# Attention followed by an MLP on one core: one dealt list of TensorE instructions for a slot's value products, transposes and scores

## The chip, the core and the metric

The kernel runs on one core of a Trainium2 chip, as one launch. The time is that of the launch on the device in microseconds (us); lower is better. The core has five engines that run side by side, each with its own instruction queue: TensorE (PE in the profile; it multiplies matrices and transposes), VectorE (DVE), ScalarE (ACT), GpSimd (POOL) and SyncE (SP, which here only starts transfers). Engines wait for each other through semaphores. A product on TensorE is two instructions in the trace: a load of the stationary operand ("weights", on the row PEld), and a matmul that streams the moving operand past it (on the row PE). Products write to PSUM, which this kernel uses as two accumulator banks of the MLP and six banks that rotate among all other tiles.

## The reference, cut to what matters

```python
# q, k, v: (8, 8, 576, 64)   f: (8, 8, 576)
scores = matmul(q, k.T) / 8
cum = cumsum(log(clip(f, 1e-4, 1)), axis=-1)
scores = where(causal, -1e9, scores + cum[..., :, None] - cum[..., None, :])
attn = exp(scores - max(scores)); attn = attn / (sum(attn) + 1e-9)
x = matmul(attn, v)                      # 64 heads, then laid out as (8, 576, 512)
xn = (x - mean(x)) / sqrt(var(x) + 1e-6) * g_ln
out = x + maximum(xn @ w_ch1, 0) @ w_ch2 # 512 -> 2048 -> 512, 4608 tokens
```

Operands are split into a high part (rounded to the format in which TensorE takes them) and a low part (the rest), and the products high x high, high x low and low x high are summed. So most products stand in the program two or three times.

## The kernel before, in words

The program is one list of slots (L770). A slot is a head `n` and a row tile `t` in 1 to 4; tile `t` holds 128 query rows, and with `t` = 1 go the head's first 64 rows as tile 0 (L295). Because of the causal mask tile `t` needs only the first 64, 192, 320, 448 or 576 keys for `t` = 0 to 4.

For each slot the letters of a string in `ORDERS` (L53) call `piece`, and each letter emits the instructions of one step. From slot 70 on the string is `WwAthQFlMSPNgreamLRDB`. Every engine runs its instructions in the order in which they are emitted. The steps that matter here:

- **A**, `av_unit` (L499): products of attention rows with v for a finished pair of row tiles; only in slots whose older tile is 2 or 4. For tile 2 they are `ph1` products with streams of 320, 256 and 128 columns and `pl1` products with 256 and 128; for tile 4 `ph2` products with four times 256 and once 128, and `pl2` products with three times 256 and once 128. A `ph` product loads 128 columns of weights (v high and v low side by side), a `pl` product 64 columns (v high alone).
- **t**, `transpose_unit` (L448): transposes of normalised rows. The rows are the weights here (64 or 128 columns loaded), and the identity streams 128 columns. Tile 1 has two transposes with 64 columns loaded and one with 128; tile 2 one and two; tile 3 one and three; tile 4 one, three, and one more into a bank of its own (`tr_4b`).
- **Q**, `qk_mm` (L363): scores of the newest tile. Each score tile is two products, `hi` x `hi` (L374) and `kl` x `xq` (L375). They load 128 columns and stream 320 (`t` = 2), 448 (`t` = 3) or twice 288 (`t` = 4). For `t` = 1 there are two score tiles: tile 0 loads 64 columns and streams 64, tile 1 loads 128 and streams 192.
- **M** and **N**, `mm1` and `mm2`: one step of the MLP. M is 12 products with 128 columns loaded and a 256-column stream (L604 to L606), N is 6 with 128 loaded and a 512-column stream (L626 to L628). N is the last TensorE work of a slot, so a 512-column stream stands ahead of the next slot's A or t; in some slots four transposes of MLP rows (`xp`, L649) stand between.
- **h** and **l** (L490, L494) take the transposes out of PSUM on ACT and DVE; **F** (L548) copies half of the value product on ACT; **S** (L388) masks the scores and takes their row extremes on DVE.

For heads from 18 on (`MOVED`, L33) the normalised rows go through a DMA into a tile `pq` before they are transposed, and a head's transposes come four slots after its scores (`LAG_MOVED`), its value products five. So a slot of head `n` with `t` = 1 holds: value products of head `n-2`, tile 4; transposes of head `n-1`, tile 1; scores of head `n`, tiles 0 and 1. With `t` = 3 it holds the value products for tile 2 of head `n-1`, the transposes of its tile 3 and the scores of tile 3. With `t` = 2 and 4 there are transposes and scores alone.

Of the kernel before, what the change touches and what calls it, by code (L numbers as in the profile page):

```python
# [9 lines left out]
F32R = mybir.dt.float32r  # L10
# [21 lines left out]
LAG, LAG_MOVED = 2, 4  # L32
# [28 lines left out]
def attn_moe(ctx: ExitStack, tc: tile.TileContext, qk, v, f, g, w1, w2, out):  # L61
    nc = tc.nc
# [9 lines left out]
    mm = nc.tensor.matmul  # L72

    def bank(name):
        return ps.tile([P, 512], F32, tag="b", bufs=6, name=name)
# [5 lines left out]
    identr = const.tile([P, P], F32R, tag="identr", name="identr")  # L81
# [3 lines left out]
    ident = identr.bitcast(F32)  # L85
# [276 lines left out]

    def qk_mm(h, t):  # L363
        q0, m, w = QT[t]
        cuts = [(0, w)] if w <= 512 else [(0, w // 2), (w // 2, w)]
        h.s = getattr(h, "s", {})
        h.s[t] = []
        for i, (a, z) in enumerate(cuts):
            sp = bank(f"s{h.n}_{t}_{i}")[:m, : z - a]
            xq, kl = h.xq[:, q0 : q0 + m], h.kl[:, a:z]  # L370
            if h.plain:
                mm(sp, xq, kl, start=True, stop=True)  # L372
            else:
                mm(sp, h.hi[:, 0, q0 : q0 + m], h.hi[:, 1, a:z], start=True, stop=False)  # L374
                mm(sp, xq, kl, start=False, stop=True)  # L375
            h.s[t].append((a, z, sp))

    corners = []

# [54 lines left out]
    def rows_of(h, t):  # L434
        return h.moved.get(t, h.p[t][0])

    def tr(out_, in_):
        m = in_.shape[0]
        if in_.dtype == F32R:
            nc.tensor.transpose(out_.bitcast(F32R), in_, identr[:m, :m])  # L440
        else:
            nc.tensor.transpose(out_, in_, ident[:m, :m])  # L442

# [2 lines left out]
    def transpose_unit(h, t):  # L448
        n = f"{h.n}"
        pt = rows_of(h, t)  # L450
        work_ = []
        if t <= 2:
            if t == 1:
                h.ph1 = work.tile([P, 704], F32 if h.full else F32R, tag="ph1", bufs=1, name=f"ph1_{n}")
                h.pl1 = None if h.full else late.tile([P, 384], F32R, tag="pl1", bufs=1, name=f"pl1_{n}")
            ph = h.ph1
            pl = ph if h.full else h.pl1
            tp = bank(f"tr{n}_{t}")
            if t == 1:
                tr(tp[0:64, 0:128], rows_of(h, 0)[:, 0:D])  # L460
                tr(tp[0:64, 64:192], pt[:, 0:64])
                tr(tp[:, 192:320], pt[:, 64:192])
                work_.append((tp[0:64, 0:192], ph[0:64, 0:192], ph[64:128, 0:192]))
                work_.append((tp[:, 192:320], ph[:, 320:448], pl[:, 0:128]))
            else:
                tr(tp[0:64, 0:128], pt[:, 0:64])
                tr(tp[:, 128:256], pt[:, 64:192])
                tr(tp[:, 256:384], pt[:, 192:320])
                work_.append((tp[0:64, 0:128], ph[0:64, 192:320], ph[64:128, 192:320]))
                work_.append((tp[:, 128:384], ph[:, 448:704], pl[:, 128:384]))  # L470
        else:
            if t == 3:
                h.ph2 = work.tile([P, 9 * P], F32 if h.full else F32R, tag="ph2", bufs=1, name=f"ph2_{n}")
                h.pl2 = None if h.full else late.tile([P, 7 * P], F32R, tag="pl2", bufs=1, name=f"pl2_{n}")
            c = 0 if t == 3 else P
            ph = h.ph2[:, : 8 * P].rearrange("p (k c) -> p k c", k=4)[:, :, c : c + P]
            pl = None if h.full else h.pl2[:, : 6 * P].rearrange("p (k c) -> p k c", k=3)[:, :, c : c + P]
            tp = bank(f"tr{n}_{t}").rearrange("p (k c) -> p k c", k=4)
            tr(tp[0:64, 0, :], pt[:, 0:64])
            for k in range(1, 4):  # L480
                tr(tp[:, k, :], pt[:, 64 + P * (k - 1) : 64 + P * k])
            work_.append((tp[0:64, 0, :], ph[0:64, 0, :], ph[64:128, 0, :]))
            work_.append((tp[:, 1:4, :], ph[:, 1:4, :], pl))
            if t == 4:
                tp = bank(f"tr{n}_4b")[:, :P]
                tr(tp, pt[:, 64 + 3 * P : 64 + 4 * P])
                work_.append((tp, h.ph2[:, 8 * P :], None if h.full else h.pl2[:, 6 * P :]))
        h.parts = work_

    def transposed_hi(h, t):  # L490
        for tp, hi, lo in h.parts:
            nc.scalar.copy(out=hi, in_=tp)  # L492
# [5 lines left out]

    def av_unit(h, t):  # L499
        po = bank(f"o{h.n}_{t}")  # L500

        if h.full:
            def fac(o, k, mv, first=False):
                st, mv = (h.vr[0:64, 0], mv[0:64]) if k == 0 else (h.vr[:, k], mv)
                mm(o, st, mv, start=first, stop=True, skip_group_check=True)  # L505

            if t == 2:
                ph = h.ph1
                fac(po[0:64, 0:320], 0, ph[:, 0:320], True)
                fac(po[0:64, 64:320], 1, ph[:, 320:576])  # L510
                fac(po[0:64, 192:320], 2, ph[:, 576:704])
                h.o = (po, S1, 0)
            else:
                ph = h.ph2
                for k in range(4):
                    fac(po[0:64, 0:256], k, ph[:, 256 * k : 256 * k + 256], k == 0)
                fac(po[0:64, 128:256], 4, ph[:, 8 * P :])
                h.o = (po, S - S1, S1)
            return

        vv = h.vv

        def both(k):
            return vv[:, k].rearrange("p a d -> p (a d)")

        def acc(o, st, mv, first=False):
            mm(o, st, mv, start=first, stop=True, skip_group_check=True)  # L527

        if t == 2:
            ph, pl, w, c0 = h.ph1, h.pl1, S1, 0  # L530
            acc(po[:, 0:320], both(0), ph[:, 0:320], True)
            acc(po[:, 64:320], both(1), ph[:, 320:576])
            acc(po[:, 192:320], both(2), ph[:, 576:704])
            acc(po[0:64, 64:320], vv[:, 1, 0, :], pl[:, 0:256])
            acc(po[0:64, 192:320], vv[:, 2, 0, :], pl[:, 256:384])
        else:
            ph, pl, w, c0 = h.ph2, h.pl2, S - S1, S1
            for k in range(4):
                acc(po[:, 0:256], both(k), ph[:, 256 * k : 256 * k + 256], k == 0)
            acc(po[:, 128:256], both(4), ph[:, 8 * P :])  # L540
            for k in range(1, 4):
                acc(po[0:64, 0:256], vv[:, k, 0, :], pl[:, 256 * (k - 1) : 256 * k])
            acc(po[0:64, 128:256], vv[:, 4, 0, :], pl[:, 6 * P :])
        h.o = (po, w, c0)

    xs_tile = {}

# [225 lines left out]
    hd = {}  # L773
# [12 lines left out]
    for u, slot in enumerate(slots):  # L786
# [4 lines left out]
        if slot is not None:  # L791
            n, t = slot
            h = hd[n]
        def turn(more):

            for lag in (LAG, LAG_MOVED):
                b = before(lag + more)
                if b is not None and hd[b[0]].lag == lag:
                    return b
            return None  # L800

        av, av_t = None, 0
        if turn(1) is not None and turn(1)[1] in (2, 4):
            av, av_t = hd[turn(1)[0]], turn(1)[1]
        moe.fetch_low(ALL if wp.done() else wp.ready())
        want = moe.can(wp.ready()) and u >= FIRST_MOE

        def piece(c):
            tu = turn(0)
            if c == "t" and tu is not None:  # L810
                transpose_unit(hd[tu[0]], tu[1])
            elif c == "h" and tu is not None:
                transposed_hi(hd[tu[0]], tu[1])
            elif c == "l" and tu is not None:
                transposed_lo(hd[tu[0]])
            elif c == "Q" and slot is not None:
                if t == 1:
                    qk_mm(h, 0)
                qk_mm(h, t)
            elif c == "A" and av is not None:  # L820
                av_unit(av, av_t)
            elif c == "S" and slot is not None:
                if t == 1:
                    softmax_a(h, 0)
# [65 lines left out]
        for c in [o for first, o in ORDERS if first <= u][-1]:  # L890
            piece(c)
# [48 lines left out]
```

## Time and profile before

| | |
|---|---|
| time before, median of 3 runs | 1207.02 us (1204.66 to 1209.07) |
| time of the profiled execution | 1205.75 us |
| its span, first to last instruction | 1204.0 us |
| transposes of heads from 18 on | 275.0 to 997.1 us of the span |
| POOL busy | 426.1 us |

The span has three parts: a beginning with weights being prepared and the first 18 heads, the stretch from 275 to 997 us with heads 18 to 63 and the MLP in alternation, and an end of 207 us with the MLP alone. The views used are the page, the busy times by windows, and the timeline of the two TensorE rows. In a timeline row stand the start, the duration, the engine, the line, the operation with its tiles, the rows and columns of the weights (128*64 is 64 columns loaded), the shape of the moving operand, and the count of merged instructions.

### The profile page before, as it was taken

How to read it: one execution, taken by the hardware profiler on the slowest of the kernel's cores; microseconds unless marked ns; L12 is line 12 of the kernel's file. 1: busy time of each engine (PE TensorE's matmuls, PEld its weight loads, DVE VectorE, ACT ScalarE, POOL GpSimd, SP SyncE). 2: the span in 40 equal slices, each digit the busy share in tenths (PEclk: the TensorE clock that was granted, in tenths of full speed). 3: DMA queues.
4: the chain of work that ended last, by engine and by line, in shares of the span. 5: the costliest groups of instructions: out<-in, count | busy, mean ns of one | idle time of the engine just before them, and what ended most of it. 6: DMA issues, size and time to landing. Idle time of an engine off the chain costs nothing.

```text
span 1204.0 us, 25987 instructions
## 1 busy us (share of the span) xinstructions
PE 1185.4 (98%) x8140; PEld 1057.7 (88%) x8140; DVE 756.5 (63%) x2884; ACT 643.2 (53%) x1920; POOL 426.1 (35%) x533
## 2 busy tenths in 40 slices
PE   7998999999999999999999999999999999999998
PEld 5666889999999999989999999999999999999997
DVE  5787647676768676766767676767676764233232
ACT  5888655565656565556565555556565642112111
POOL 3568544343434434344434433434444320000000
PEclk8999999999999999999999999999999999999999
DMA  7788653557666767567676666657666654434433
GB/s 204 228 239 272 204 163 118 154 172 214 219 202 202 234 187 231 170 217 218 212 224 199 209 207 205 221 181 231 199 220 213 189 182 135 128 121 126 139 108 94
DMA packets 171481, 228.50 MB, mean 190 GB/s; under 512 B 40784, under 2 KB 107856, under 8 KB 171344
## 3 DMA queue, kind: packets, MB, share of 16 engines
q1 hardware_dynamic: 171344, 226.85, 60.7%
q8 instruction: 65, 1.06, 0.4%
q14 instruction: 72, 0.59, 0.1%
HBM read 157.46 MB, written 23.36 MB: 150 GB/s over the span
## 4 chain that ended last, share of the span: by engine, by line
PE 92%; DVE 3%; ACT 2%; DMA 2%; issue 1%; SPq 0%; POOL 0%; DVEq 0%; ACTq 0%; POOLq 0%
PE h L604 11%; PE h L605 11%; PE h L606 11%; PE acc L626 11%; PE acc L627 11%; PE acc L628 11%; PE o L527 6%; PE s L374 4%; PE tr L440 4%; PE s L375 3%; PE o L505 3%; PE tr L442 2%; PE s L372 2%; PE xp L649 1%; PE pc L191 1%
## 5 line engine op out<-in xcount | busy, mean ns | idle before, releaser
L416 POOL TENSOR_SCALAR p<-p,st 64x64 f32<-64x64 f32 (+4 forms) x320 | 172.5, 543 | 489.4 <-DVE st L415 196.7
L604 PE MATMUL h<-x,w1h 128*128 128x256 f32 x1152 | 330.0, 286 | 0.8 <-ACT xs L558 0.8
L605 PE MATMUL h<-x,w1h 128*128 128x256 f32 x1152 | 325.6, 283 | 1.4 <-DVE st L414 1.3
L606 PE MATMUL h<-x,w1l 128*128 128x256 f32 x1152 | 325.3, 282 | 0.0
L612 ACT ACTIVATE hh<-h 128x256 fp32r<-128x256 f32 x288 | 110.3, 383 | 303.3 <-PE h L606 303.0
L617 DVE SCALAR_TENSOR_TENSOR hh<-h,hh 128x256 fp32r<-128x256 f32 x288 | 121.1, 421 | 172.9 <-ACT hh L612 170.9
L626 PE MATMUL acc<-w2h,hh 128*128 128x512 f32 x576 | 226.6, 393 | 0.0
L627 PE MATMUL acc<-w2s,hh 128*128 128x512 f32 x576 | 226.4, 393 | 0.0
L628 PE MATMUL acc<-w2h,hh 128*128 128x512 f32 x576 | 225.1, 391 | 0.0
L604 PEld LDWEIGHTS h<-x,w1h 128*128 128x128 f32 x1152 | 218.8, 190 | 6.2 <-ACT xs L558 1.0
L605 PEld LDWEIGHTS h<-x,w1h 128*128 128x128 f32 x1152 | 219.2, 190 | 5.2 <-DVE x L589 2.0
L606 PEld LDWEIGHTS h<-x,w1l 128*128 128x128 f32 x1152 | 219.2, 190 | 0.0
L409 ACT ACTIVATE p<-p,st 64x64 f32<-64x64 f32 (+4 forms) x320 | 178.3, 558 | 49.2 <-DVE st L398 45.6
L492 ACT CAST ph<-tr 64x128 fp32r<-64x128 f32 (+4 forms) x416 | 117.8, 332 | 130.9 <-PE tr L440 76.5
L398 DVE CUSTOM_DVE_ANT_0 p<-s,mask 64x64 f32<-64x64 f32 (+4 forms) x320 | 130.7, 420 | 17.0 <-DMA pq<-p 5.2
L497 DVE TENSOR_TENSOR ph<-tr,ph 64x192 fp32r<-64x192 f32 x208 | 62.6, 301 | 108.7 <-ACT ph L492 83.6
L628 PEld LDWEIGHTS acc<-w2h,hh 128*128 128x128 f32 x576 | 108.2, 188 | 24.1
L626 PEld LDWEIGHTS acc<-w2h,hh 128*128 128x128 f32 x576 | 109.4, 190 | 12.6
L627 PEld LDWEIGHTS acc<-w2s,hh 128*128 128x128 f32 x576 | 109.3, 190 | 11.8
L374 PE MATMUL s<-hi 128*64 128x64 f32 x336 | 105.4, 336 | 1.3 <-POOL hi L352 1.0
L497 DVE TENSOR_TENSOR pl<-tr,ph 128x128 fp32r<-128x128 f32 x208 | 95.3, 458 | 4.6
L375 PE MATMUL s<-kl,xq 66*64 66x64 f32 x336 | 98.0, 296 | 0.0
(86 smaller groups left out, 1784.5 us busy)
## 6 DMA issues: line engine op xcount, KB each, us to landing
w2s<-w2d SPq DMA_DIRECT2D x288, 256.0 KB
raw<-in_qk_dram SPq DMA_DIRECT2D x56, 576.0 KB
wr<-in_w_dram SPq DMA_DIRECT2D x32, 512.0 KB
pq<-p SPq DMA_DIRECT2D x46, 288.0 KB
pq<-p SPq DMA_DIRECT2D x46, 224.0 KB
vr<-in_v_dram SPq DMA_DIRECT2D x64, 160.0 KB
out_dram<-xt SPq DMA_DIRECT2D x36, 256.0 KB
xq<-hi SPq DMA_DIRECT2D x56, 144.0 KB
```

The lines of the kernel that those rows point to most:

```text
L374: mm(sp, h.hi[:, 0, q0 : q0 + m], h.hi[:, 1, a:z], start=True, stop=False)
L375: mm(sp, xq, kl, start=False, stop=True)
L398: nc.vector.tensor_tensor_reduce(out=pt[:m, a:z], in0=sp, in1=mask[:m, off + a : off + z], scale=-SCALE, scalar=3.0e38 if i == 0 else st[: ...
L409: nc.scalar.activation(pt[:m, :w], pt[:m, :w], AF.Exp, bias=st[:m, i : i + 1], scale=-1.0, accum_out=st[:m, 2:3])
L416: nc.gpsimd.tensor_scalar(out=pt[:m, :w], in0=pt[:m, :w], scalar1=st[:m, 3:4], scalar2=1.0, op0=ALU.mult, op1=ALU.mult)
L497: nc.vector.tensor_tensor(out=lo, in0=tp, in1=hi.bitcast(F32), op=ALU.subtract)
L604: mm(ph, w1h[:, k, fs], c.x[k][:, 0, :], start=(k == 0), stop=False)
L605: mm(ph, w1h[:, k, fs], c.x[k][:, 1, :], start=False, stop=False)
L606: mm(ph, w1l[:, k, fs], c.x[k][:, 0, :], start=False, stop=(k == KT - 1))
L626: mm(c.acc[i], h[:, 0, ts_], w2h[:, j, :], start=(j == 0), stop=False)
L627: mm(c.acc[i], h[:, 0, ts_], low, start=False, stop=False)
L628: mm(c.acc[i], h[:, 1, ts_], w2h[:, j, :], start=False, stop=(j == FT - 1))
```

## The change

`qk_mm`, `transpose_unit` and `av_unit` no longer emit their products and transposes; each returns a list of them. For heads with the lag of four, the letter A now builds all three lists (and allocates their PSUM banks in the order of before), deals them into one list with a new function `dealt`, and emits that; the letters t and Q then emit nothing. Earlier heads run their lists as they come.

```diff
     def qk_mm(h, t):
         q0, m, w = QT[t]
+        todo = []
+
+        def mm(*a, **k):
+            todo.append(lambda: nc.tensor.matmul(*a, **k))
...
+    def dealt(t, u1, a, b, q):
+
+        if t == 4 and q:
+            return a[:5] + a[8:] + b[:2] + q[:1] + a[5:6] + b[2:] + q[1:2] + a[6:7] + q[2:3] + a[7:8] + q[3:]
+        if t == 4:
+            return a[:5] + a[8:] + b[:2] + a[5:6] + b[2:] + a[6:8]
+        if t == 2:
+            return a[:3] + a[4:] + b + a[3:4] + q
+        return (a + b if u1 else b[1:] + b[:1]) + q
...
         def piece(c):
             tu = turn(0)
-            if c == "t" and tu is not None:
-                transpose_unit(hd[tu[0]], tu[1])
+            if c in "AtQ" and tu is not None and hd[tu[0]].lag == LAG_MOVED:
+                if c == "A":
+                    a = av_unit(av, av_t) if av is not None else []
+                    b = transpose_unit(hd[tu[0]], tu[1])
+                    q = []
+                    if slot is not None:
+                        q = (qk_mm(h, 0) if t == 1 else []) + qk_mm(h, t)
+                    run(dealt(av_t, tu[1] == 1, a, b, q))
+            elif c == "t" and tu is not None:
+                run(transpose_unit(hd[tu[0]], tu[1]))
...
             elif c == "A" and av is not None:
-                av_unit(av, av_t)
+                run(av_unit(av, av_t))
```

In `dealt`, `a` are the value products, `b` the transposes, `q` the score products; its `t` is the tile of the value products (0 where there are none).

The rows below are TensorE's instructions in order: line, tile written, tiles read, and the shape of the result (partitions x columns streamed). Names carry the head: `o28_4` is the value product of head 28 for tile 4, `tr29_1` the transposes of head 29's tile 1, `s30_1_0` scores of head 30's tile 1, `h` and `acc` the MLP. First a slot with `t` = 1, on TensorE, before, from the last `ph` product on:

```order
L527 MATMUL o28_4_6646<-ph2_28_6526,vv28_6428 128x128
L527 MATMUL o28_4_6646<-pl2_28_6527,vv28_6428 64x256 x3
L527 MATMUL o28_4_6646<-pl2_28_6527,vv28_6428 64x128
L440 MATMUL tr29_1_6658<-identr_74,pq29_0_6511 64x128
L440 MATMUL tr29_1_6658<-identr_74,pq29_1_6513 64x128
L440 MATMUL tr29_1_6658<-identr_74,pq29_1_6513 128x128
L374 MATMUL s30_0_0_6664<-hi30_6422 64x64
L375 MATMUL s30_0_0_6664<-kl30_6423,xq8_1143 64x64
L374 MATMUL s30_1_0_6667<-hi30_6422 128x192
L375 MATMUL s30_1_0_6667<-kl30_6423,xq8_1143 128x192
L604 MATMUL h5_0_6675<-x5_0_6172,w1h_124 128x256
```

and the same slot with the change, from the `pl` product that comes first now:

```order
L513 MATMUL o28_4_6646<-pl2_28_6522,vv28_6428 64x128
L456 MATMUL tr29_1_6649<-identr_74,pq29_0_6511 64x128
L456 MATMUL tr29_1_6649<-identr_74,pq29_1_6513 64x128
L368 MATMUL s30_0_0_6650<-hi30_6422 64x64
L513 MATMUL o28_4_6646<-pl2_28_6522,vv28_6428 64x256
L456 MATMUL tr29_1_6649<-identr_74,pq29_1_6513 128x128
L368 MATMUL s30_0_0_6650<-kl30_6423,xq8_1143 64x64
L513 MATMUL o28_4_6646<-pl2_28_6522,vv28_6428 64x256
L368 MATMUL s30_1_0_6651<-hi30_6422 128x192
L513 MATMUL o28_4_6646<-pl2_28_6522,vv28_6428 64x256
L368 MATMUL s30_1_0_6651<-kl30_6423,xq8_1143 128x192
L628 MATMUL h5_0_6675<-x5_0_6172,w1h_124 128x256
```

The three `pl` products with 256-column streams have moved from ahead of the transposes to between transposes and scores, and the one with 128 columns stands ahead of them. Next a slot with `t` = 3 on TensorE, before, from the last `ph` product on:

```order
L527 MATMUL o29_2_6780<-ph1_29_6656,vv29_6699 128x128
L527 MATMUL o29_2_6780<-pl1_29_6657,vv29_6699 64x256
L527 MATMUL o29_2_6780<-pl1_29_6657,vv29_6699 64x128
L440 MATMUL tr29_3_6788<-identr_74,pq29_3_6639 64x128
L440 MATMUL tr29_3_6788<-identr_74,pq29_3_6639 128x128 x3
L374 MATMUL s30_3_0_6795<-hi30_6422 128x448
L375 MATMUL s30_3_0_6795<-kl30_6423,xq8_1143 128x448
```

and with the change:

```order
L513 MATMUL o29_2_6780<-ph1_29_6647,vv29_6699 128x128
L513 MATMUL o29_2_6780<-pl1_29_6648,vv29_6699 64x128
L456 MATMUL tr29_3_6783<-identr_74,pq29_3_6639 64x128
L456 MATMUL tr29_3_6783<-identr_74,pq29_3_6639 128x128 x3
L513 MATMUL o29_2_6780<-pl1_29_6648,vv29_6699 64x256
L368 MATMUL s30_3_0_6784<-hi30_6422 128x448
L368 MATMUL s30_3_0_6784<-kl30_6423,xq8_1143 128x448
```

The `pl` product with the 256-column stream has moved behind the transposes. Last a slot with `t` = 2 on TensorE, before, behind the MLP's last product:

```order
L626 MATMUL acc5_1_6760<-w2h_126,hh5_4_6953 128x512
L627 MATMUL acc5_1_6760<-w2s84_6837,hh5_4_6953 128x512
L628 MATMUL acc5_1_6760<-w2h_126,hh5_4_6953 128x512
L440 MATMUL tr30_2_6970<-identr_74,pq30_2_6832 64x128
L440 MATMUL tr30_2_6970<-identr_74,pq30_2_6832 128x128 x2
L374 MATMUL s31_2_0_6976<-hi31_6693 128x320
L375 MATMUL s31_2_0_6976<-kl31_6694,xq9_1286 128x320
```

and with the change:

```order
L652 MATMUL acc5_1_6760<-w2h_126,hh5_4_6953 128x512
L456 MATMUL tr30_2_6970<-identr_74,pq30_2_6832 128x128 x2
L456 MATMUL tr30_2_6970<-identr_74,pq30_2_6832 64x128
L368 MATMUL s31_2_0_6971<-hi31_6693 128x320
L368 MATMUL s31_2_0_6971<-kl31_6694,xq9_1286 128x320
```

The transpose that loads 64 columns has moved behind those that load 128; `t` = 4 is dealt in the same way. The order on DVE, ACT, POOL and SP is that of before.

More of the change, by code (lines that the diff above doesn't have):

```diff
@@ L376, in qk_mm @@
             h.s[t].append((a, z, sp))
+        return todo
     corners = []
@@ L435, in rows_of @@
         return h.moved.get(t, h.p[t][0])
[L437 to L442, printed above, removed]
     def transpose_unit(h, t):
@@ L450, in transpose_unit, with tr @@
         pt = rows_of(h, t)
-        work_ = []
+        work_, todo = [], []
+        def tr(out_, in_):
+            m = in_.shape[0]
+            if in_.dtype == F32R:
+                todo.append(lambda: nc.tensor.transpose(out_.bitcast(F32R), in_, identr[:m, :m]))
+            else:
+                todo.append(lambda: nc.tensor.transpose(out_, in_, ident[:m, :m]))
         if t <= 2:
@@ L488, in transpose_unit @@
         h.parts = work_
+        return todo
     def transposed_hi(h, t):
@@ L500, in av_unit, with mm @@
         po = bank(f"o{h.n}_{t}")
+        todo = []
+        def mm(*a, **k):
+            todo.append(lambda: nc.tensor.matmul(*a, **k))
         if h.full:
@@ L518, in av_unit @@
                 h.o = (po, S - S1, S1)
-            return
+            return todo
         vv = h.vv
@@ L544, in av_unit @@
         h.o = (po, w, c0)
+        return todo
+    def dealt(t, u1, a, b, q):
[6 more added lines that the diff above has]
+        return (a + b if u1 else b[1:] + b[:1]) + q
     xs_tile = {}
@@ L806, in attn_moe, with run @@
         want = moe.can(wp.ready()) and u >= FIRST_MOE
+        def run(todo):
+            for emit in todo:
+                emit()
         def piece(c):
             tu = turn(0)
-            if c == "t" and tu is not None:
-                transpose_unit(hd[tu[0]], tu[1])
+            if c in "AtQ" and tu is not None and hd[tu[0]].lag == LAG_MOVED:
[8 more added lines that the diff above has]
+                run(transpose_unit(hd[tu[0]], tu[1]))
             elif c == "h" and tu is not None:
@@ L816, in piece @@
             elif c == "Q" and slot is not None:
-                if t == 1:
-                    qk_mm(h, 0)
-                qk_mm(h, t)
+                run((qk_mm(h, 0) if t == 1 else []) + qk_mm(h, t))
             elif c == "A" and av is not None:
-                av_unit(av, av_t)
+                run(av_unit(av, av_t))
             elif c == "S" and slot is not None:
```

## The prediction

> **What bounds the kernel now.** The page first: busy times, and the chain of work that ended last.
>
> ```profile
> span 1204.0 us, 25987 instructions
> ...
> PE 1185.4 (98%) x8140; PEld 1057.7 (88%) x8140; DVE 756.5 (63%) x2884; ACT 643.2 (53%) x1920; POOL 426.1 (35%) x533
> ...
> PE 92%; DVE 3%; ACT 2%; DMA 2%; issue 1%; SPq 0%; POOL 0%; DVEq 0%; ACTq 0%; POOLq 0%
> ```
>
> TensorE is the bound: 98% busy and 92% of the chain. Next, where the changed instructions run (the transposes' tile `pq`), and the busy times of that stretch by windows.
>
> ```profile
> L440 PE MATMUL tr<-identr,pq x644: 220/231/300, 275.0 to 997.1; 128*128 128x128 f32 x92, 128*64 128x128 f32 x69
> L440 PE MATMUL tr_4b<-identr,pq x46: 246/247/248, 286.2 to 997.2; 128*128 128x128 f32 x46
> ...
> 275.00:997.00 722.00, 719.89 (x5210) 662.98 (x5208) 507.48 (x1987) 423.94 (x1289) 284.26 (x360) 1.00 0.66 207
> ```
>
> `tr_4b` is made once a head: 46 heads. In their 722 us PE is busy 719.89, so all its waiting there is 2.1 us; the next engine, DVE, is busy 507.48, or 70%. The granted clock is 1.00. Only TensorE's own stream of instructions can move this stretch. But a busy PE row does not say that it streams all the time, so the third view is the timeline of the weight loads. A slot with `t` = 2, from the load under the MLP's last 512-column stream on:
>
> ```profile
> 626.28 0.11 PEld L440 LDWEIGHTS tr<-identr,pq 128*64 128x64 f32 x1
> 626.51 0.14 PEld L440 LDWEIGHTS tr<-identr,pq 128*128 128x128 f32 x1
> 626.60 0.14 PEld L440 LDWEIGHTS tr<-identr,pq 128*128 128x128 f32 x1
> 626.68 0.19 PEld L374 LDWEIGHTS s<-hi 128*128 128x128 f32 x1
> 626.79 0.19 PEld L375 LDWEIGHTS s<-kl,xq 66*128 66x128 f32 x1
> 626.94 0.19 PEld L604 LDWEIGHTS h<-x,w1h 128*128 128x128 f32 x1
> 627.09 0.19 PEld L605 LDWEIGHTS h<-x,w1h 128*128 128x128 f32 x1
> ```
>
> I read the start of a load as the moment when the product before it takes over the array, since only then can the next weights be loaded behind it. The distance of two starts is then the longer of two things: the stream of the product that runs, and the load that goes on behind it. 626.28 to 626.51 is the 512-column stream (0.23). 626.51 to 626.60 to 626.68 cannot be streams, as I show next, so they are loads of 128 columns for a transpose: 0.085 each. 626.68 to 626.79 is a load of 128 columns for a product: 0.11. The last two steps, 0.15, are the 320-column streams. A slot with `t` = 1 gives the other prices:
>
> ```profile
> 622.64 0.43 PEld L527 LDWEIGHTS o<-pl,vv 128*64 128x64 f32 x4
> 623.05 0.26 PEld L440 LDWEIGHTS tr<-identr,pq 128*64 128x64 f32 x3
> 623.26 0.13 PEld L374 LDWEIGHTS s<-hi 128*64 128x64 f32 x1
> 623.31 0.14 PEld L375 LDWEIGHTS s<-kl,xq 66*64 66x64 f32 x1
> 623.37 0.19 PEld L374 LDWEIGHTS s<-hi 128*128 128x128 f32 x1
> 623.48 0.19 PEld L375 LDWEIGHTS s<-kl,xq 66*128 66x128 f32 x1
> 623.59 0.19 PEld L604 LDWEIGHTS h<-x,w1h 128*128 128x128 f32 x1
> 623.71 0.19 PEld L605 LDWEIGHTS h<-x,w1h 128*128 128x128 f32 x1
> ```
>
> The transpose with 128 columns loaded takes over at 623.26 and its 128-column stream is through by 623.31: so a 128-column stream is no longer than 0.06, and the 0.085 above were loads. 623.31 to 623.37 is a load of 64 columns behind a 64-column stream: 0.057. The next three steps, 0.11 each, are loads of 128 columns behind streams of 64, 192 and 192. **Short streams with large loads behind them are where TensorE is held up.** A slot with `t` = 3 prices the streams:
>
> ```profile
> 630.54 0.13 PEld L527 LDWEIGHTS o<-pl,vv 128*64 128x64 f32 x1
> 630.60 0.13 PEld L527 LDWEIGHTS o<-pl,vv 128*64 128x64 f32 x1
> 630.72 0.11 PEld L440 LDWEIGHTS tr<-identr,pq 128*64 128x64 f32 x1
> 631.03 0.19 PEld L374 LDWEIGHTS s<-hi 128*128 128x128 f32 x1
> 631.14 0.19 PEld L375 LDWEIGHTS s<-kl,xq 66*128 66x128 f32 x1
> ```
>
> With 64 columns to load, a 128-column stream takes 0.06 (630.54 to 630.60) and a 256-column one 0.12 (630.60 to 630.72). So a load of 128 columns (0.11) is hidden behind 256 columns and sticks out 0.05 behind 128; one of 64 columns (0.057) is hidden behind 128.
>
> **The change part by part.** No instruction is added or removed; TensorE's order alone changes, in heads 18 to 63. Below, ns per step, each the longer of stream and load.
>
> *`t` = 2.* Before, from the takeover of the first transpose to that of the scores: 85 + 85 + 110 = 280 (the rows: 626.51 to 626.79). After, the first 128-column load lies behind the 512-column stream and costs nothing; then 85 (second), 60 (the 64-column one, hidden behind a 128-column stream), 110 (scores): 255. Saved 25. *`t` = 4* has two more transposes and the same ends: saved 25. That a first 128-column load vanishes behind 512 columns is seen where MLP rows are transposed:
>
> ```profile
> 629.68 0.14 PEld L649 LDWEIGHTS xp<-identr,xw 128*128 128x128 f32 x1
> 629.91 0.14 PEld L649 LDWEIGHTS xp<-identr,xw 128*128 128x128 f32 x1
> ...
> 630.08 0.14 PEld L649 LDWEIGHTS xp<-identr,xw 128*128 128x128 f32 x1
> 630.17 0.19 PEld L527 LDWEIGHTS o<-ph,vv 128*128 128x128 f32 x1
> ```
>
> 629.68 to 629.91 is the bare 0.23. By the order of the program two slots of each kind have these transposes ahead instead and save nothing: 44 slots each, 44 x 2 x 25 = 2.2 us.
>
> *`t` = 3.* Before, from the last `ph` product's takeover to that of the scores: 60 + 120 + 60 + 3 x 85 + 110 = 605 (rows: 630.54 to 631.14, 600). After: `pl` 60, transposes 60 + 3 x 85, then the `pl` product's 64 columns behind a transpose, 60, and the scores' 128 columns behind its 256, 120: 555. Against the rows that saves 45, against the steps 50; I take 47. 46 slots, 2.2 us.
>
> *`t` = 1.* Before, from the last `ph` product on: 60, 3 x 120, 60, 60, 85, 57, 57, 110, 110, 110 = 1069 (rows: 622.64 to 623.71, 1.07). After, in the order of the new rows: `pl` 60, transposes 60 and 60, score 60, `pl` behind a 64-column stream 57, transpose 120, score 60, `pl` 57, score 120, `pl` behind a 192-column stream 90 (three quarters of 120, an estimate from the 256-column step), score 120, MLP 110 = 974. Saved 95; 44 slots, 4.2 us; the last head's slot without scores some 0.1.
>
> Sum: 2.2 + 2.2 + 4.2 + 0.1 = **8.7 us**, off the path in full, since nothing else holds PE in this stretch. What is late next:
>
> ```profile
> 639.59 0.47 ACT L492 CAST ph<-tr 64x192 fp32r<-64x192 f32 x2 [0.77 <-PE s L374]
> 640.09 0.37 ACT L561 COPY ot<-o 64x256 f32<-64x256 f32 x1
> ...
> 636.54 0.28 DVE L497 TENSOR_TENSOR pl<-tr_4b,ph 128x128 fp32r<-128x128 f32 x1
> ...
> 638.73 0.58 PE L527 MATMUL o<-pl,vv 128*64 128x256 f32 x4
> ...
> L527 PE MATMUL o<-pl,vv x272: 221/278/298, 282.1 to 993.6; 128*64 128x256 f32 x136
> ```
>
> ACT's copy of the value product now waits for the last moved `pl` product. Behind it in ACT's queue stand the copy of the next head's rows, the MLP's first copy and that slot's exponentials, for which DVE and POOL wait. By the steps above that `pl` product takes over 0.68 after the first one (at 638.73 in these rows), and products of its shape last 0.28 (the last row, the median): done at about 639.7, ahead of the 640.09 at which ACT comes to the copy today; the casts ahead of it start 0.2 earlier, as the transposes do. So I cost the wait at nothing; without the cover of 0.4 ACT would lose what goes beyond 640.09, and it is 59% busy here. The `pl` product that now comes first reads what DVE ends at 636.82, 1.9 us earlier. DMAs, and the queues of SP and POOL, keep their order.
>
> Not shown before: score and value products in alternation. The bounds: nothing (tr to score took 57, no more than its load), or the whole load exposed, 57, at each added change of kind. I take nothing, the nearest rows.
>
> The whole sum rests on loads that hide behind streams: from 623.59 to 623.71 the MLP's first 256-column stream (0.12) and a load of 128 columns (0.11) pass in 0.12. The Trainium skill, "TensorE: Matmul & The Clock Gate", Part 3, "The mechanism", says that a load overlaps with a running matmul only where their row groups differ; both of these use all 128 rows and overlap, so the trace disagrees, and what the rule would give here is rival (d).
>
> **The rivals.** (a) *The transposes are slow themselves*: 85 wherever they stand, and 25 more at their end. Then `t` = 2, 3 and 4 save nothing and `t` = 1 some 70 (95 less the 25 at its transpose): 44 x 70 = 3.1 us, 1202.7. For it: the steps of `t` = 2 alone would read the same. Against it: 623.26 to 623.31.
>
> (b) *Slower: each change of kind (value product, transpose, score) exposes the load that comes with it*, in the slots with `t` = 1, which go from 3 such changes to 10, and by one in `t` = 3: 44 x 7 + 46 = 354 more. At 57 each that is 20.2 us, less 8.7: 11.5 slower, 1217.3. It decides from 25 ns a change. Against it: the changes there are (value product to transpose, transpose to score, score to MLP) show bare loads and streams.
>
> (c) *The gain is met elsewhere*: transfers or DVE hold PE as soon as it runs ahead; 1205.8. Against it: 2.1 us of waits in 722.
>
> (d) *Loads do not hide behind streams, so that order is worth nothing*: each step a sum, stream + load. The same loads and streams then add up in any order: 1205.8. Against it: 256 columns with a load of 128 would take 0.12 + 0.11, and take 0.12.
>
> **How the numbers follow.** The profiled execution took 1205.75, its span and 1.75 around it that the change does not touch; 1205.75 - 8.7 = 1197.05. It lies 1.3 below the median of 1207.02, which gives 1198.3 from there; I take the middle, **1197.7**. Chances: forecast 0.74; half the gain, with the steps in alternation longer than I think, 1201.4, 0.08; (a) 0.06; (b) 0.05; (c) 0.05; (d) 0.02. The three runs of before spread from 2.4 below to 2.0 above their median, so the forecast itself is 1195 to 1200.5; the range, with half the gain and (a), is **1195 to 1203**. A difference of 0.3% (3.6 us) is about what a measurement of this kernel can tell from no change. Faster: forecast and half, 0.82; within: (a), (c), (d), 0.13; slower: (b), 0.05.
>
> **What would show it.** The stretch of the `pq` transposes, 722 us, comes out at 713, with PE still busy all through; the 207 us behind it stay. In a slot with `t` = 1 the way from the last `ph` product to the MLP is 0.97, not 1.07, with no step over 0.12; in `t` = 3, 0.555 to the scores; in `t` = 2, the first step behind 0.23 belongs to a second 128-column transpose. Wrong would be: moved `pl` products at 0.11 or more behind 64-column streams (b), the 64-column transpose in `t` = 2 at 0.085 (a), or new waits of PE for DVE, ACT or DMA (c).

## The result, and the profile after

| | before | with the change |
|---|---|---|
| median of the runs | 1207.29 us (4 runs, 1204.66 to 1209.07) | 1199.09 us (4 runs, 1198.67 to 1200.18) |
| span of the profiled execution | 1204.0 us | 1196.9 us |

The ratio is 0.9935, with a 95% interval from 0.9916 to 0.9955: 5.4 to 10.1 us less, 7.8 in the middle. 8.7 us were forecast, and 1197.7 us.

The page and the views of the changed kernel that answer to those of before: busy times, the transposes' tile `pq`, the busy times by windows, and the waits of PE in the stretch.

```profile
span 1196.9 us, 26079 instructions
...
PE 1176.4 (98%) x8140; PEld 1050.7 (88%) x8140; DVE 758.8 (63%) x2884; ACT 643.6 (54%) x1920; POOL 426.0 (36%) x533
...
L456 PE MATMUL tr<-identr,pq x644: 220/227/280, 275.5 to 990.1; 128*128 128x128 f32 x115, 128*64 128x128 f32 x46
...
275.00:990.00 715.00, 712.25 (x5212) 656.61 (x5210) 509.45 (x1988) 424.69 (x1291) 284.34 (x360) 1.00 0.66 209
990.00:1197.00 207.00, 202.99 (x1321) 184.48 (x1318) 61.55 (x188) 38.08 (x98) 0.00 (x0) 1.00 0.40 123
...
PE h L629 <- DVE st L420: 1.0, 1, 1.0
PE tr L456 <- DMA pq<-p: 0.9, 1, 0.9
PE o L513 <- DVE ph L506: 0.4, 1, 0.4
PE s L368 <- DVE st L404: 0.3, 1, 0.3
```

The work is the same, 8140 products. The stretch of the `pq` transposes went from 722.1 to 714.6 us; the 207 us behind it stayed. PE is busy in 712.25 of 715, its waits are four, and the other engines' busy times are those of before within half a per cent. So the time came out of TensorE's own stream, though its instruction list holds the same loads and matmuls. Most of it is due to the order; up to 1 us of the 7.5 is not, as the head near 515 us shows below.

How it came out is read from the weight loads. A slot with `t` = 1 of the changed kernel, timeline of the loads (columns as before), from the first `pl` product's load on:

```profile
650.53 0.13 PEld L513 LDWEIGHTS o<-pl,vv 128*64 128x64 f32 x1
650.61 0.17 PEld L456 LDWEIGHTS tr<-identr,pq 128*64 128x64 f32 x2
650.72 0.13 PEld L368 LDWEIGHTS s<-hi 128*64 128x64 f32 x1
650.78 0.14 PEld L513 LDWEIGHTS o<-pl,vv 128*64 128x64 f32 x1
650.86 0.14 PEld L456 LDWEIGHTS tr<-identr,pq 128*128 128x128 f32 x1
650.96 0.14 PEld L368 LDWEIGHTS s<-kl,xq 66*64 66x64 f32 x1
651.02 0.14 PEld L513 LDWEIGHTS o<-pl,vv 128*64 128x64 f32 x1
651.08 0.19 PEld L368 LDWEIGHTS s<-hi 128*128 128x128 f32 x1
651.20 0.13 PEld L513 LDWEIGHTS o<-pl,vv 128*64 128x64 f32 x1
651.28 0.19 PEld L368 LDWEIGHTS s<-kl,xq 66*128 66x128 f32 x1
651.40 0.19 PEld L628 LDWEIGHTS h<-x,w1h 128*128 128x128 f32 x1
651.51 0.19 PEld L629 LDWEIGHTS h<-x,w1h 128*128 128x128 f32 x1
```

The start of a load is again read as the takeover of the product ahead of it. 650.53 is the takeover of the last `ph` product, 651.51 that of the MLP's first: 0.98, where it was 1.07 to 1.08. The 128-column loads of scores start at 651.08 and 651.28, under the 256-column streams of the `pl` products ahead of them, and the steps to the next starts are 0.12, no more than those streams. The 64-column loads behind 64-column streams are over in 0.08 (650.78 to 650.86) and 0.06 (651.02 to 651.08).

### The profile page after: what moved, and what is told of

The parts are those of the page before. It is cut to its first block, busy times and chain, and to the rows that moved or that the text cites. A ratio compares the mean times of both kernels' runs of the same rounds, so it can differ in the third digit from the quotient of the medians.

```text
span 1196.9 us, 26079 instructions
## 1 busy us (share of the span) xinstructions
PE 1176.4 (98%) x8140; PEld 1050.7 (88%) x8140; DVE 758.8 (63%) x2884; ACT 643.6 (54%) x1920; POOL 426.0 (36%) x533
## 4 chain that ended last, share of the span: by engine, by line
PE 67%; DVE 1%; DMA 1%; issue 0%; SPq 0%; DVEq 0%
PE h L628 9%; PE h L629 9%; PE h L630 9%; PE acc L650 9%; PE acc L651 9%; PE acc L652 9%; PE s L368 5%; PE o L513 5%; PE tr L456 3%; PE xp L673 1%; DMA pq<-p 1%; DVE xt L709 0%; PE tr_4b L456 0%; DVE p L404 0%; DVE pl L506 0%
## 5 line engine op out<-in xcount | busy, mean ns | idle before, releaser
L368 PE MATMUL s<-hi 128*64 128x64 f32 x336 | 101.6, 311 | 1.3 <-POOL hi L352 1.0
L368 PE MATMUL s<-kl,xq 66*64 66x64 f32 x336 | 95.5, 289 | 0.0
```

Source lines behind the costliest of these rows:

```text
L368: todo.append(lambda: nc.tensor.matmul(*a, **k))
```

## The experiments

All kernels below differ from the changed one in `dealt` alone. The ways through a slot are medians over some 35 to 43 slots of a kind, from the starts of the loads; times are compared with runs of before on the same chip. How many us less a kernel takes is worked out from the ratio, which has the interval in brackets; the difference of the two medians is up to 1.2 us away from it. Where heads are compared, a head is the time from the MLP's first load behind one slot with `t` = 1 to that behind the next, the same head in both traces, one trace for each kernel. Heads in which PE waits (near 385 and 515 us, and one near 810 us in two of the traces) are left out.

### The parts alone

First, only slots with `t` = 2 and 4 dealt:

```diff
     def dealt(t, u1, a, b, q):
 
-        if t == 4 and q:
...
-            return a[:3] + a[4:] + b + a[3:4] + q
+        if t:
+            return a + b + q
         return (a + b if u1 else b[1:] + b[:1]) + q
```

> Only the slots without value products (t = 2 and 4) are dealt: the 64-column transpose last. Theory (a load is hidden behind a long stream and sticks out behind a short one): in a t = 2 slot the way from the takeover of the first transpose to that of the scores falls from 0.28 to 0.25, in 44 slots of each kind; 2.2 to 2.7 us less than before, 1203 to 1205 by the time of before. Rival (transposes with 128 columns are slow themselves, wherever they stand): 0.28 stays, and the time of before, 1205 to 1207.

Measured: 1204.11 us against 1205.62, ratio 0.9994 (0.9981 to 1.0006). In the slots the theory held: from the takeover of the first transpose to that of the scores 0.248 instead of 0.279 with `t` = 2, and 0.417 instead of 0.452 with `t` = 4. Over the whole slots, from the takeover of the MLP's last product to that of the next step's first, medians again, it is 0.030 and 0.039, 3.0 us over 44 of each kind. (The 0.061 in an expectation below counts on to the step's third product.) So the transposes are not slow themselves: their first load is paid or hidden. But only 0.7 us of it arrived in the time, with an interval that takes in nothing; head by head it is 0.023 in the mean, 1.1 us over 46 heads. Where most of it went is seen in the MLP step behind the slot, 18 products. Timeline of the loads of this kernel: the starts that mark the takeover of the step's first product and of its last:

```profile
665.45 0.19 PEld L625 LDWEIGHTS h<-x,w1h 128*128 128x128 f32 x1
...
668.07 0.19 PEld L513 LDWEIGHTS o<-ph,vv 128*128 128x128 f32 x1
```

By these rounded rows it is 2.62, behind `t` = 4. There the median was 2.574 before, and in this kernel 36 of 45 steps take 2.61. Behind `t` = 3 it rose from 2.576 to 2.593. The slots whose order was left alone moved too: with `t` = 1 the whole slot is 0.016 shorter than before, with `t` = 3 it is 0.009 longer. So one slot's way depends by some 0.01 on what ran ahead of it.

Second, only `t` = 1 dealt: the last two returns become `return a + b + q`.

> Only the slots with t = 1 are dealt. Theory: from the takeover of the last ph product to that of the MLP 0.98 instead of 1.07 to 1.08, 44 slots, 4.0 to 4.2 us less than before, about half of what the whole change gave. Rival (the gain comes mostly from the transposes' order in the other slots): under 2 us less.

Measured: 1201.18 us, ratio 0.9964 (0.9952 to 0.9976), 4.3 us less. The slot's way is 0.98 instead of 1.08, and the MLP steps behind it kept their length. This part is more than half of the gain.

Third, only `t` = 3 dealt: the first two returns are left out, the last becomes `return a + b + q`.

> Only the slots with t = 3 are dealt. From the takeover of the last ph product to that of the scores 0.56 instead of 0.59, 1.3 us less than before by these steps. Two theories on the MLP step behind these slots, which took 2.61 instead of 2.58 in most of them with the whole change: if the dealt order of this slot makes it, it is 2.61 here too, and of the 1.3 us only some 0.5 are left; if the earlier slots make it, it stays 2.58 and 1.3 us are left.

Measured: 1204.73 us, ratio 0.9990 (0.9980 to 1.0000), 1.2 us less, with an interval that ends at nothing; head by head it is 1.2 us too. From the last `ph` product to the scores 0.560 instead of 0.590. The MLP step behind took 2.59 in 31 of 46 slots and 2.58 in 13: longer by 0.01 to 0.02, not by 0.03. So neither theory has it: the dealt order of this slot does not by itself make 2.61.

### The same alternation with spoiled pairs

```diff
         if t == 4 and q:
-            return a[:5] + a[8:] + b[:2] + q[:1] + a[5:6] + b[2:] + q[1:2] + a[6:7] + q[2:3] + a[7:8] + q[3:]
+            return a[:5] + a[5:6] + a[8:] + q[:1] + a[6:7] + b[:1] + q[1:2] + a[7:8] + b[1:2] + q[2:3] + b[2:] + q[3:]
```

> The change, but in slots with t = 1 the same products, transposes and scores stand in an order with as many changes of kind (10) and the pairs spoiled: 128-column loads stand behind 64- and 128-column streams again, and the 256-column streams are spent on 64-column loads. Theory (pairs of stream and load decide): from the last ph product to the MLP 1.07, as before the change, 4 us slower than the change. Rival (alternation as such shortens the slot, since value products no longer stand in a row): as fast as the change, 0.98. Rival (alternation costs): slower than 1.08.

Measured: 1203.38 us, ratio 0.9984 (0.9973 to 0.9996), 2 us less than before where the change gave 7.8. Timeline of the loads: takeover of the last `ph` product, then the end of the slot:

```profile
668.73 0.13 PEld L513 LDWEIGHTS o<-pl,vv 128*64 128x64 f32 x1
...
669.39 0.19 PEld L368 LDWEIGHTS s<-hi 128*128 128x128 f32 x1
669.52 0.14 PEld L456 LDWEIGHTS tr<-identr,pq 128*128 128x128 f32 x1
669.61 0.19 PEld L368 LDWEIGHTS s<-kl,xq 66*128 66x128 f32 x1
669.72 0.19 PEld L628 LDWEIGHTS h<-x,w1h 128*128 128x128 f32 x1
669.83 0.19 PEld L629 LDWEIGHTS h<-x,w1h 128*128 128x128 f32 x1
```

1.10 from 668.73 to 669.83, against 0.98 with the change and 1.08 before. The same twelve products in as many changes of kind take 0.12 longer when the 128-column loads stand behind short streams again; alternation alone gains nothing. It is 0.02 over the way of before: the load of the last transpose, behind a product of scores, starts 0.13 after that product's load and not 0.11 (669.39 to 669.52). The next experiments are about such late loads.

### Where the changed slots are longer than the sum

In the changed slot above, the step behind the first `pl` product is 0.08 (650.53 to 650.61), not 0.06. Two theories, and one edit:

```diff
-            return a[:5] + a[8:] + b[:2] + q[:1] + a[5:6] + b[2:] + q[1:2] + a[6:7] + q[2:3] + a[7:8] + q[3:]
+            return a[:5] + b[:1] + a[8:] + b[1:2] + q[:1] + a[5:6] + b[2:] + q[1:2] + a[6:7] + q[2:3] + a[7:8] + q[3:]
...
-            return a[:3] + a[4:] + b + a[3:4] + q
+            return a[:3] + b[:1] + a[4:] + b[1:] + a[3:4] + q
```

> The change, with one thing more: in slots with t = 1 and 3 the 64-column transpose stands between the last ph product and the pl product that streams 128 columns, where the change has these two products in a row. With the change the ph product's takeover to that of the pl product, and on to that of the transpose, takes 0.132 to 0.136 in the load starts, against 0.12 by the prices (two streams of 128 columns). Theory 1 (two products in a row that add to the same 128 columns of a bank hold each other up): the three steps are 0.06 each, 0.014 saved in 90 slots, 1.2 us faster than the change. Theory 2 (the load that waits for a semaphore comes late): the step over 0.06 stays with the transpose or moves with it, and nothing is saved.

Measured: 1199.36 us against 1199.30 for the change on the same chip (ratio to before 0.9946, 0.9930 to 0.9962). Nothing was saved; the slot with `t` = 3 even takes 0.01 more, and head by head this kernel saves 5.9 us where the change saves 6.8. Theory 1 falls. A `t` = 3 slot of this kernel, loads:

```profile
658.71 0.19 PEld L513 LDWEIGHTS o<-ph,vv 128*128 128x128 f32 x1
658.84 0.11 PEld L456 LDWEIGHTS tr<-identr,pq 128*64 128x64 f32 x1
658.90 0.13 PEld L513 LDWEIGHTS o<-pl,vv 128*64 128x64 f32 x1
658.98 0.31 PEld L456 LDWEIGHTS tr<-identr,pq 128*128 128x128 f32 x3
```

The transpose's load now starts 0.13 behind the `ph` product's, where 0.118 is usual there, and the next transpose's load 0.08 behind that of the `pl` product, though nothing adds to the same columns next to it any more. Nor is it the wait on a semaphore, since the load at 658.98 has none. What the late loads have in common is a transpose behind a product. But not every load of that kind is late: the first transpose of before stands behind a `pl` product too, and its load starts 0.12 after that product's (630.60 to 630.72 in the rows of the prediction), just the 256-column stream that runs there. The late loads start some 0.02 after the load ahead of them could be over: 0.08 behind a load of 64 columns (0.057), 0.13 behind one of 128 (0.11). This is a reading of these traces; no run varied the load ahead alone. One more order was tried for this, with three such places in `t` = 3:

```diff
-            return a[:3] + a[4:] + b + a[3:4] + q
+            return a[:3] + b[:1] + a[4:] + b[1:3] + a[3:4] + b[3:] + q
```

> The change, with the slots of t = 3 in an order that goes three times from a product to a transpose, twice of them behind 128-column streams: ph product, transpose (64), pl (128), transpose, transpose, pl (256), transpose, scores. Theory from the last runs (the load of a transpose that comes behind a product starts 0.02 late, which shows unless the product streams 256 columns): from the last ph product's takeover to that of the scores 0.070, 0.060, 0.105, 0.085, 0.060, 0.120, 0.110 = 0.61; loads of the first transpose and of the one behind the pl product with 128 columns start 0.015 to 0.03 after the matmul ahead of them instead of 0.003. Rival (loads and streams alone, no cost of a change of kind): 0.58. Against 0.56 with the change, so about 2 us slower than the change by the theory and 1 by the rival.

Loads of a `t` = 3 slot of that kernel:

```profile
659.07 0.19 PEld L513 LDWEIGHTS o<-ph,vv 128*128 128x128 f32 x1
659.20 0.11 PEld L456 LDWEIGHTS tr<-identr,pq 128*64 128x64 f32 x1
659.25 0.13 PEld L513 LDWEIGHTS o<-pl,vv 128*64 128x64 f32 x1
659.33 0.23 PEld L456 LDWEIGHTS tr<-identr,pq 128*128 128x128 f32 x2
659.50 0.13 PEld L513 LDWEIGHTS o<-pl,vv 128*64 128x64 f32 x1
659.58 0.14 PEld L456 LDWEIGHTS tr<-identr,pq 128*128 128x128 f32 x1
659.68 0.19 PEld L368 LDWEIGHTS s<-hi 128*128 128x128 f32 x1
659.79 0.19 PEld L368 LDWEIGHTS s<-kl,xq 66*128 66x128 f32 x1
```

The `ph` product takes over at 659.19 (659.07 and a 256-column stream of 0.12), the scores at 659.79: 0.60 to 0.61, as the theory of late loads had it, not 0.58. (The medians give 0.605: 0.59 from the first transpose's load on, and the 0.014 by which that load is late.) All three loads of transposes behind products come late (0.13 for 0.118, twice 0.08 for 0.06), and only the one behind 256 streamed columns costs nothing: from 659.50 to 659.68, 0.18, is a 64-column load and a 256-column stream. The time is 1200.84 us, ratio 0.9953 (0.9933 to 0.9973); between 1 and 2 us more than the change it cannot tell. Head by head it saves 4.8 us where the change saves 6.8, the 2 us of the theory.

### What is saved in the slots of transposes, and the whole against its parts

```diff
-        return (a + b if u1 else b[1:] + b[:1]) + q
+        return (a + b if u1 else b[1:2] + b[:1] + b[2:]) + q
```

> The change, but in slots with t = 2 and 4 the 64-column transpose stands second instead of last. Theory (what is saved is the first 128-column load, behind the 512-column stream): the steps are 0.06, 0.085, 0.11 where the change has 0.085, 0.055, 0.11, from first takeover to scores 0.25, as with the change. Rival (the saving comes from having the smaller transpose ahead of the scores' load): 0.28, as before, and 2.6 us slower than the change.

Measured: 1198.15 us, ratio 0.9936 (0.9918 to 0.9955), like the change. With `t` = 2 the steps are 0.060, 0.085, 0.108, together 0.253 against 0.248 with the change and 0.279 before. The place of the small transpose hardly matters (0.005); a 128-column load under the 512-column stream does.

> The changed kernel itself once more, for a narrower interval and beside the next three: 7 to 8.5 us less than before.

Measured: 1199.30 us, ratio 0.9942 (0.9924 to 0.9959), 7.0 us less.

For the last one, `t` = 2 and 4 stand as before (`return a + b + q` at the end):

> The change without its part for t = 2 and 4, whose slots stand as before. Alone that part saved 0.061 a head in its own slots (2.7 us) and only 0.7 in the time, since the MLP steps behind t = 4 went from 2.58 to 2.61. If that loss belongs to the part, this kernel is within 1 us of the change; if the loss depends on the whole program's timing, it is 2 to 3 us slower than the change and 4.5 to 6 faster than before.

Measured: 1200.14 us, ratio 0.9956 (0.9941 to 0.9970): 5.3 us less than before. By the ratios it is 1.7 us slower than the change measured beside it, by the medians 0.8. The intervals overlap, so by the times it stays open whether the part for `t` = 2 and 4 brings 2 to 3 us or under 1 inside the whole. Head by head this kernel is 0.117 shorter than before and the change 0.149, 5.4 and 6.8 us over 46 heads: 1.4 us for the part in these two traces.

## Why the prediction was right, point by point

**The bound** held: PE alone sets this stretch, its waits are 2.75 us (2.1 before), and the 207 us behind did not move. One thing in it was overlooked: the granted clock of 1.00 is rounded. The kernel before, busy times behind a wait of PE (the third number from the end is the granted clock):

```profile
517.80:521.20 3.40, 3.40 (x17) 3.32 (x16) 1.34 (x5) 1.47 (x5) 2.61 (x3) 0.50 0.99 379
```

For 3.4 us TensorE ran at half its clock. In the first trace of the changed kernel this does not happen in the stretch; in its second trace it does, once, from 519.5 us on and for as long. Why it comes in some runs is open.

**The reading of load starts** held, and with it the prices 0.057, 0.085, 0.11, and 0.06 and 0.12 for the streams. By slot, as medians of the load starts:

| slot | forecast saving | measured, whole slot to the takeover of the MLP's first product | MLP step behind, before to after |
|---|---|---|---|
| `t` = 1 | 0.095 | 0.097 | 2.583 to 2.587 |
| `t` = 2 | 0.025 | 0.033 | 2.585, the same |
| `t` = 3 | 0.047 | 0.028 | 2.576 to 2.610 |
| `t` = 4 | 0.025 | 0.028 | 2.574 to 2.583 |
| a head | 0.192 | 0.186 | 0.047 longer |

The head's period went from 15.64 to 15.50 us, 0.14 less: 0.186 less 0.047. Heads with transposes of MLP rows in their slots gained 0.10 to 0.21 each. In the mean it is 0.149 a head, 6.8 us over 46 heads, and in the second trace of the change 6.9. The first trace's stretch gained 7.5, mostly since one more head, near 515 us, took 17.62 us before, with the half clock in it, and 16.47 with the change; in the second trace the same head took 18.59. So what the order is worth is some 6.8 us. That the time came out as near to the forecast as 7.8 is partly luck; its interval, 5.4 to 10.1, holds 6.8 as well as 8.7.

**Two terms were mis-sized.** In `t` = 3 I took 0.047 and it is 0.028. The slot whose rows I quoted had MLP transposes ahead; in an ordinary slot the way before was shorter. Loads of such a slot in the kernel before, the one that marks the `ph` product's takeover and the one that marks the scores':

```profile
677.51 0.19 PEld L527 LDWEIGHTS o<-pl,vv 128*64 128x64 f32 x2
...
678.10 0.19 PEld L375 LDWEIGHTS s<-kl,xq 66*128 66x128 f32 x1
```

The same way in the changed kernel:

```profile
657.96 0.13 PEld L513 LDWEIGHTS o<-pl,vv 128*64 128x64 f32 x1
658.04 0.36 PEld L456 LDWEIGHTS tr<-identr,pq 128*64 128x64 f32 x4
658.35 0.13 PEld L513 LDWEIGHTS o<-pl,vv 128*64 128x64 f32 x1
658.40 0.19 PEld L368 LDWEIGHTS s<-hi 128*128 128x128 f32 x1
658.52 0.19 PEld L368 LDWEIGHTS s<-kl,xq 66*128 66x128 f32 x1
```

0.59 before, not 0.60; 0.56 after. The "nothing" that I took for alternation is, for a transpose behind a product with 128 streamed columns, some 0.015 (step 657.96 to 658.04, 0.08 for 0.06, of which the next step gives a little back). Once in each slot with value products, 90 slots, it makes about 1.3 us, inside the bounds I gave and under the 0.025 for every change of kind from which rival (b) decides. In `t` = 1 the way is 0.982 by the medians, not 0.974, and the saving is still what was forecast only since the way before was longer than its sum too, 1.079 for 1.069. That the two misses cancel is luck.

The second is a term that stood in no sum: the MLP step between the slots, held equal. Behind `t` = 3 it grew. The kernel before, from the load start that marks the takeover of the step's first product to that of its last:

```profile
662.87 0.19 PEld L605 LDWEIGHTS h<-x,w1h 128*128 128x128 f32 x1
...
665.45 0.11 PEld L440 LDWEIGHTS tr<-identr,pq 128*64 128x64 f32 x1
```

The same two marks with the change:

```profile
658.94 0.19 PEld L629 LDWEIGHTS h<-x,w1h 128*128 128x128 f32 x1
...
661.55 0.14 PEld L456 LDWEIGHTS tr<-identr,pq 128*128 128x128 f32 x1
```

2.58 and 2.61. Over a head the MLP steps took back 0.047 of 0.186, some 2 us of the 8.7. The longer step is not new: in the kernel before, the nine steps behind `t` = 3 with transposes of MLP rows ahead of the slot took 2.61 each.

**What was to be late next**, ACT's copy of the value product, was not: ACT has no idle time ahead of it in the changed trace. The one longer wait of PE is 0.9 us for a transfer of `pq`, once.

**The rivals.** (a), slow transposes, falls by the slots dealt alone (0.248 for 0.279) and by the order with the small transpose second. (b), exposed loads at each change of kind, is true of one kind of change, at a quarter of the price. (c) came only in small: the waits grew by 0.65 us, most of it once; in the second trace of the change PE waited 2.5 us for transfers of `pq`, twice. (d) falls with the spoiled pairs, which give the whole gain of `t` = 1 back with the same loads and streams.

## What to carry to other kernels

A busy TensorE row does not show that it streams: the distance between the starts of weight loads does, and each is the longer of the stream that runs and the load behind it. Count short streams and small loads before reordering; the gain is what long loads save when they move from behind short streams to behind long ones, here 0.05 us a pair. Two other orders with nearly the same pairs (`e5_apart`, `e6_mid`) came out within some 1 us of the change. Compare the traces piece by piece, too: one wait or one stretch at half the clock can be worth a sixth of such a gain. Sum the changed slots, but also measure the work between them, since it need not stay equal.

## What was not expected of the hardware

- A transpose's load behind a product starts about 0.02 us after the load ahead of it could be over (0.08 between load starts behind 64 columns, 0.13 behind 128). It costs nothing where a 256-column stream ahead outlasts that, as in the kernel before (0.12), or where the product behind which it lies streams 256 columns itself. Transposes behind transposes, and products behind transposes, showed no such cost.
- The same 18 products of an MLP step take 2.57 to 2.61 us in the stretch of the slots, by kernel and slot. In the end of the program, with the MLP alone, nearly every one of them takes 2.58, before as after. The changed kernel profiled a second time had 28 of 45 steps behind `t` = 3 at 2.61, where the first had 36, so the order of the program does not settle it alone. What does stays open: neither the other engines' traffic nor the moment of entry was varied by itself.
